# Two chained feed-forward layers behind pooled attention: matmuls that read each stream by turns from its two halves

## The chip, the cores and the metric

The kernel runs on one core of a Trainium2 chip. The metric is the device time of one execution in microseconds (us); the kernel before takes 964.29 us, the median of three runs (964.23 to 964.79).

## What is computed

12480 tokens of 128 features go through an attention with 32 inducing points, then through two feed-forward layers of width 2048, all in float32:

```python
h = mab(I, x)                     # 32 rows: softmax(scale * I x^T) x
x = mab(x, h)                     # 12480 rows: softmax(scale * x h^T) h
h1 = x @ w_in;  x = maximum(0.01 * h1, h1) @ w_out
h2 = x @ w2_in; x = (h2 * sigmoid(1.702 * h2)) @ w2_out
```

## The kernel before, in words

Tokens are the columns everywhere: a tile of tokens is 128 partitions (features, or rows of attention weights) by 512 columns. There are 25 such tiles; the last two in the order of work have 352 columns. The first 40 us or so pool the tokens into the 32 rows (transposes, scores, a running softmax). Then come two layers of 25 tiles by 16 steps, 800 steps in all, in the order of the list `steps`: layer 1 for all tiles, then layer 2 for all tiles, and within a tile the 16 blocks f of 128 hidden features. The program is written out in that order by hand; `extra` hangs other work (weight conversion, attention weights of later tiles, splitting) on chosen steps.

One step has three parts. `ffn_in` multiplies a block of the first matrix with the tile's stream into a PSUM tile `h_ps`; `ffn_act` applies the nonlinearity and splits the result into two float32r streams `ghi` (rounded) and `glo` (the rest); `ffn_out`, three steps later (`LOOK`), multiplies them with the second matrix and adds to the tile's PSUM tile `acc`. A product of two float32 factors is made of three float32r matmuls: high by high, low by high, high by low.

- Layer 1, inward: one matmul (L774), `hw` by `at`. The attention is folded into the first matrix (`hw`), and the stream `at` holds the attention weights of the tile's tokens; for the first two tiles ScalarE writes it (L580), for the others `stack` loads it with four DMAs (L662), ten steps before it is first read.
- Layer 1, activation: ScalarE's relu writes `ghi` (L788), VectorE writes `glo` (L789).
- Layer 2, inward: three matmuls (L778, L779, L780) on `x2h` and `x2l`, which `halves` splits from the first layer's result (L514 on ScalarE, L515 on VectorE).
- Layer 2, activation: ScalarE's silu (L794) and its rounding copy `ghi` (L795), VectorE's `glo` (L796).
- Outward, both layers: L806, L807 (both on `ghi`) and L808 (on `glo`); at the last step of a tile of layer 1 one more, `lin` by `at` (L810), which carries the 0.01 part of the first nonlinearity.
- `ffn_end` copies `acc` out: in layer 1 to `x2` on ScalarE (L824); in layer 2 to `o_t` on VectorE (L832), for the very last tile on ScalarE (L829), followed by the store.

In a matmul the streamed operand (`at`, `x2h`, `x2l`, `ghi`, `glo`) is called the stream or moving operand here, the matrix block that is loaded into the array the weights. All streams are read in the order of their columns.

Of the kernel before, what the change touches and what calls it, by code (L numbers as in the profile page):

```python
# [10 lines left out]
F32 = mybir.dt.float32  # L11
F32R = mybir.dt.float32r
U32 = mybir.dt.uint32
BF16 = mybir.dt.bfloat16
AF = mybir.ActivationFunctionType
# [3 lines left out]
P = 128  # L19
LOOK = 3  # L20
# [37 lines left out]
def kernel(  # L58
# [12 lines left out]
    nc = tc.nc  # L71
    _, N, C = x.shape
    m = inducing.shape[0]
    DFF = moe_w_in.shape[1]
    NF = DFF // P
    TOK = TC * P
# [3 lines left out]
    tok = [TC * k for k in ch]  # L80
# [7 lines left out]
    const = ctx.enter_context(tc.tile_pool(name="const", bufs=1))  # L88
# [151 lines left out]
    while len(early) < len(order):  # L240
# [6 lines left out]
        out=sel, in_=ident.rearrange("p (q k) -> p k q", q=NQ), axis=AX.X, op=ALU.add  # L247
# [7 lines left out]
        out=quad, in_=ident.rearrange("p (q k) -> p q k", q=NQ), axis=AX.X, op=ALU.add  # L255
# [6 lines left out]
    l = xnp.tile([P, NP], F32, name="l")  # L262
# [7 lines left out]
    def slot(t, dtype, name):  # L270
        return slots.tile([P, TOK], dtype, tag=f"slot{t}", name=f"{name}{t}")
# [151 lines left out]
    for i in range(NP - 1):  # L423
# [10 lines left out]
        j = 0 if i == 1 else i - 2 if i >= 3 else None  # L434
# [69 lines left out]
    main = ctx.enter_context(tc.tile_pool(name="main", bufs=2))  # L504
# [2 lines left out]

    main.tile([P, 112], F32, tag="gap", name="gap", bufs=1)

    def halves(src, name, pool=const, tag=None):  # L510
        shape = list(src.shape)
        hi = pool.tile(shape, F32R, name=f"{name}h", tag=f"{tag or name}h")
        lo = pool.tile(shape, F32R, name=f"{name}l", tag=f"{tag or name}l")
        nc.scalar.activation(out=hi, in_=src, func=AF.Copy)  # L514
        nc.vector.tensor_tensor(out=lo, in0=src, in1=hi.bitcast(F32), op=ALU.subtract)  # L515
        return hi, lo


    at_t = {}

    def weights_tile():


        return main.tile([P, TOK], F32R, tag="at", name="at", bufs=3)

    def token_tile(t, rest):

        st = {}
        n = ch[t]
        bc = lambda v: v.rearrange("p (j u) -> p j u", u=1).to_broadcast([n, TC, m])  # L530
        tiny = lambda name: main.tile([P, TC], F32, tag=name, name=name, bufs=2)[:n]

        def s0():
            ps = ps_h.tile([P, 512], F32, tag="h", name="s2_ps")
            for k in range(TC):
                nc.tensor.matmul(
                    ps[:n, k * m : (k + 1) * m], xT[t][:, k * n : (k + 1) * n],
                    hT[:, 0, :], start=True, stop=True,
                )
            st["ps"] = ps  # L540

        def s0b():
            ps = st["ps"]
            sv = ps[:n, : TC * m].rearrange("p (j k) -> p j k", j=TC)
            mxt = tiny("nmx")
            nc.vector.tensor_reduce(out=mxt, in_=sv, axis=AX.X, op=ALU.max)
            a = main.tile([P, TC, m], F32, tag="na", name="na", bufs=2)[:n]
            nc.vector.tensor_tensor(out=a, in0=sv, in1=bc(mxt), op=ALU.subtract)
            nc.scalar.activation(out=a, in_=a, func=AF.Exp, scale=SCALE)
            st["a"] = a  # L550

        def s1():
            a = st["a"]
            sst = tiny("nsum")
            nc.vector.tensor_reduce(out=sst, in_=a, axis=AX.X, op=ALU.add)
            nc.vector.tensor_scalar_add(sst, sst, EPS)
            nc.vector.reciprocal(sst, sst)
            nc.vector.tensor_tensor(out=a, in0=a, in1=bc(sst), op=ALU.mult)

        def s2():  # L560
            a = st["a"]
            rows = main.tile([P, TC, NQ, m], F32R, tag="rows", name="rows", bufs=2)[:n]
            dup = lambda v: v.rearrange("p j (u k) -> p j u k", u=1).to_broadcast(
                [n, TC, 2, m]
            )
            hi, lo = rows[:, :, 0:NQ:2, :], rows[:, :, 1:NQ:2, :]
            nc.vector.tensor_copy(hi, dup(a))
            rest.tensor_tensor(out=lo, in0=dup(a), in1=hi.bitcast(F32), op=ALU.subtract)
            st["rows"] = rows

        def s3():
            ps = ps_h.tile([P, 512], F32, tag="h", name="rows_ps")
            for k in range(TC):
                nc.tensor.transpose(
                    ps[:, k * n : (k + 1) * n],
                    st["rows"][:, k].rearrange("p q k -> p (q k)").bitcast(F32),
                    ident[:n, :n],
                )
            at_t[t] = weights_tile()[:, : tok[t]]
            nc.scalar.activation(out=at_t[t], in_=ps[:, : tok[t]], func=AF.Copy)  # L580

        return [s0, s0b, s1, s2, s3]

    NG = (NT - 2 + NQ - 1) // NQ
    hl = [None] * NG
# [71 lines left out]

    def stack(t):
        g, q = divmod(t - 2, NQ)
        a = weights_tile()[:, : tok[t]]  # L660
        for k in range(NQ):
            nc.sync.dma_start(  # L662
                out=a[k * m : (k + 1) * m, :].bitcast(F32),
                in_=hl[g][k % 2][q * m : (q + 1) * m, : tok[t]],
            )
        at_t[t] = a

# [12 lines left out]
    hw = wts.tile([P, DFF], F32R, name="hw")  # L680
# [32 lines left out]
    lin = const.tile([P, C], F32R, name="lin")  # L713
# [48 lines left out]
    x2_t = {}  # L762
    x2h_t = {}
    h_t = {}
    g_t = {}
    acc_t = {}
    late = {}

    def ffn_in(l, t, f):
        ps = ps_h.tile([P, 512], F32, tag="h", name="h_ps")  # L770
        o = ps[:, : tok[t]]
        cols = slice(f * P, (f + 1) * P)
        if l == 0:
            nc.tensor.matmul(o, hw[:, cols], at_t[t], start=True, stop=True)  # L774
        else:
            hi, lo = x2h_t[t]
            wh, wl = late["w2"]
            nc.tensor.matmul(o, wh[:, cols], hi, start=True, stop=False)  # L778
            nc.tensor.matmul(o, wl[:, cols], hi, start=False, stop=False)  # L779
            nc.tensor.matmul(o, wh[:, cols], lo, start=False, stop=True)  # L780
        h_t[l, t, f] = o

    def ffn_act(l, t, f):
        o = h_t.pop((l, t, f))
        hi = main.tile([P, TOK], F32R, tag="ghi", name="ghi", bufs=LOOK + 2)[:, : tok[t]]
        lo = main.tile([P, TOK], F32R, tag="glo", name="glo", bufs=LOOK + 2)[:, : tok[t]]
        if l == 0:
            nc.scalar.activation(out=hi, in_=o, func=AF.Relu)  # L788
            nc.vector.scalar_tensor_tensor(  # L789
                out=lo, in0=o, scalar=0.0, in1=hi.bitcast(F32), op0=ALU.max, op1=ALU.subtract  # L790
            )
        else:
            g = main.tile([P, TOK], F32, tag="g", name="g")[:, : tok[t]]
            nc.scalar.activation(out=g, in_=o, func=AF.Silu, scale=BETA)  # L794
            nc.scalar.activation(out=hi, in_=g, func=AF.Copy)  # L795
            nc.vector.tensor_tensor(out=lo, in0=g, in1=hi.bitcast(F32), op=ALU.subtract)  # L796
        g_t[l, t, f] = (hi, lo)

    def ffn_out(l, t, f):
        hi, lo = g_t.pop((l, t, f))  # L800
        if f == 0:
            acc_t[l, t] = ps_a.tile([P, 512], F32, tag="a", name="acc")
        o = acc_t[l, t][:, : tok[t]]
        v = v1 if l == 0 else late["v2"]
        end = l == 1 and f == NF - 1
        nc.tensor.matmul(o, v[:, f, 0, :], hi, start=(f == 0), stop=False)  # L806
        nc.tensor.matmul(o, v[:, f, 1, :], hi, start=False, stop=False)  # L807
        nc.tensor.matmul(o, v[:, f, 0, :], lo, start=False, stop=end)  # L808
        if l == 0 and f == NF - 1:
            nc.tensor.matmul(o, lin, at_t.pop(t), start=False, stop=True)  # L810

    def x2_slot(t):

# [6 lines left out]
    def ffn_end(l, t):  # L820
        ps = acc_t.pop((l, t))[:, : tok[t]]
        if l == 0:
            x2_t[t] = slot(x2_slot(t), F32, "x2")[:, : tok[t]]
            nc.scalar.activation(out=x2_t[t], in_=ps, func=AF.Copy, scale=1.0 - LEAK)  # L824
        else:
            o = main.tile([P, TOK], F32, tag="o", name="o_t")[:, : tok[t]]
            dst = outT[:, col[t] : col[t] + tok[t]]
            if t == NT - 1:
                nc.scalar.activation(out=o, in_=ps, func=AF.Copy, scale=1.0 / BETA)  # L829
                nc.scalar.dma_start(out=dst, in_=o)  # L830
            else:
                nc.vector.tensor_scalar_mul(o, ps, 1.0 / BETA)  # L832
                nc.sync.dma_start(out=dst, in_=o)

    steps = [(l, t, f) for l in range(2) for t in range(NT) for f in range(NF)]
    steps[: 2 * NF] = [(0, t, 4 * b + f) for b in range(NF // 4) for t in (0, 1) for f in range(4)]
# [69 lines left out]
    def split_x2(t):  # L906

        if not gaps:
            gaps.append(main.tile([P, 96], F32, tag="gap2", name="gap2", bufs=1))
        x2h_t[t] = halves(x2_t.pop(t), "x2", main)  # L910

    for t in range(NT):
        at(NT * NF + (t - 1) * NF + 6, split_x2, t)
# [1 line left out]
    for n in range(len(steps) + LOOK):  # L915
# [3 lines left out]
        if n >= LOOK:  # L919
            l, t, f = steps[n - LOOK]  # L920
# [44 lines left out]
```

## Time and profile before

| what | value |
|---|---|
| median of three runs | 964.29 us (964.23 to 964.79) |
| profiled execution, first to last instruction (its span) | 962.6 us |
| TensorE busy | 953.7 us (99%) |
| TensorE loading weights | 779.5 us (81%) |
| ScalarE busy | 783.0 us (81%) |
| VectorE busy | 631.5 us (66%) |
| GpSimd busy | 52.8 us (5%) |

The page gives the span as the profiled execution's own time. A matmul's record lasts from its start until its last result is written; records overlap, so how fast TensorE works is read from the distance between starts. PEld is the loading of weights, which runs beside the matmul before it. The granted clock is a share of TensorE's full 2.4 GHz; the lower of its two levels is 1.2 GHz. A chain of waits is followed back from the last instruction to what released each step.

### The profile page before, as it was taken

How to read it: one execution, taken by the hardware profiler on the slowest of the kernel's cores; microseconds unless marked ns; L12 is line 12 of the kernel's file. 1: busy time of each engine (PE TensorE's matmuls, PEld its weight loads, DVE VectorE, ACT ScalarE, POOL GpSimd, SP SyncE). 2: the span in 40 equal slices, each digit the busy share in tenths (PEclk: the TensorE clock that was granted, in tenths of full speed). 3: DMA queues.
4: the chain of work that ended last, by engine and by line, in shares of the span. 5: the costliest groups of instructions: out<-in, count | busy, mean ns of one | idle time of the engine just before them, and what ended most of it. 6: DMA issues, size and time to landing. Idle time of an engine off the chain costs nothing.

```text
span 962.6 us, 13196 instructions
## 1 busy us (share of the span) xinstructions
PE 953.7 (99%) x4577; PEld 779.5 (81%) x4577; DVE 631.5 (66%) x1002; ACT 783.0 (81%) x1357; POOL 52.8 (5%) x64
## 2 busy tenths in 40 slices
PE   8999999999999999999999999999999999999998
PEld 6677787887878878898888888888888888888888
DVE  3897788878878777765555555555555555555554
ACT  6666777767767666689999999999999999999998
POOL 1330101102100010000000000000000000000000
PEclk9999999999999999999999999999999999999999
DMA  9302120021000000000000000000000000000000
GB/s 337 107 1 55 34 66 23 20 81 33 23 22 12 23 12 19 8 1 12 12 12 12 12 11 12 15 19 12 12 11 12 12 12 12 12 12 23 12 12 16
DMA packets 15334, 27.90 MB, mean 29 GB/s; under 512 B 2347, under 2 KB 6987, under 8 KB 15267
## 3 DMA queue, kind: packets, MB, share of 16 engines
q1 hardware_dynamic: 15123, 26.88, 9.0%
q8 instruction: 36, 0.59, 0.3%
q14 instruction: 31, 0.25, 0.1%
q10 hardware_dynamic: 144, 0.18, 0.1%
HBM read 14.79 MB, written 6.39 MB: 22 GB/s over the span
## 4 chain that ended last, share of the span: by engine, by line
PE 94%; DVE 3%; DMA 1%; ACT 1%; issue 0%; POOL 0%; SPq 0%; ACTq 0%; POOLq 0%
PE acc L806 18%; PE acc L808 18%; PE acc L807 18%; PE h_ps L778 9%; PE h_ps L780 9%; PE h_ps L779 9%; PE h_ps L774 9%; DVE glo L789 1%; DMA xn<-in_x_dram 1%; PE s_ps L609 1%; PE xT_ps L279 1%; PE acc L810 1%; PE pv_ps L348 0%; DVE v L158 0%; DVE v L153 0%
## 5 line engine op out<-in xcount | busy, mean ns | idle before, releaser
L796 DVE TENSOR_TENSOR glo<-g,ghi 128x512 fp32r<-128x512 f32 (+1 forms) x400 | 271.7, 679 | 236.8 <-ACT ghi L795 223.2
L788 ACT ACTIVATE ghi<-h_ps 128x512 fp32r<-128x512 f32 (+1 forms) x400 | 232.2, 587 | 97.8 <-PE h_ps L774 96.2
L806 PE MATMUL acc<-ghi,v 128*128 128x512 f32 (+1 forms) x800 | 309.8, 387 | 0.0
L789 DVE SCALAR_TENSOR_TENSOR glo<-h_ps,ghi 128x512 fp32r<-128x512 f32 (+1 forms) x400 | 264.4, 674 | 68.8 <-ACT ghi L788 63.8
L808 PE MATMUL acc<-glo,v 128*128 128x512 f32 (+1 forms) x800 | 309.2, 386 | 0.1
L807 PE MATMUL acc<-ghi,v 128*128 128x512 f32 (+1 forms) x800 | 307.5, 384 | 0.0
L794 ACT ACTIVATE g<-h_ps 128x512 f32<-128x512 f32 (+1 forms) x400 | 234.3, 586 | 33.7 <-PE h_ps L780 0.6
L795 ACT ACTIVATE ghi<-g 128x512 fp32r<-128x512 f32 (+1 forms) x400 | 248.4, 621 | 12.7
L808 PEld LDWEIGHTS acc<-glo,v 128*128 128x128 f32 x800 | 150.2, 188 | 32.2 <-DVE glo L789 0.6
L807 PEld LDWEIGHTS acc<-ghi,v 128*128 128x128 f32 x800 | 150.2, 188 | 30.5
L806 PEld LDWEIGHTS acc<-ghi,v 128*128 128x128 f32 x800 | 150.3, 188 | 28.6 <-issue 0.2
L774 PE MATMUL h_ps<-at,hw 128*128 128x512 f32 (+1 forms) x400 | 155.7, 390 | 0.0
L778 PE MATMUL h_ps<-x2h,w2h 128*128 128x512 f32 (+1 forms) x400 | 155.3, 388 | 0.0
L780 PE MATMUL h_ps<-x2l,w2h 128*128 128x512 f32 (+1 forms) x400 | 154.5, 386 | 0.0
L779 PE MATMUL h_ps<-x2h,w2l 128*128 128x512 f32 (+1 forms) x400 | 153.1, 383 | 0.0
L774 PEld LDWEIGHTS h_ps<-at,hw 128*128 128x128 f32 x400 | 75.1, 188 | 18.8 <-issue 3.8
L780 PEld LDWEIGHTS h_ps<-x2l,w2h 128*128 128x128 f32 x400 | 75.1, 188 | 16.2
L779 PEld LDWEIGHTS h_ps<-x2h,w2l 128*128 128x128 f32 x400 | 75.1, 188 | 15.5
L778 PEld LDWEIGHTS h_ps<-x2h,w2h 128*128 128x128 f32 x400 | 75.2, 188 | 13.8
L824 ACT ACTIVATE x<-acc 128x512 f32<-128x512 f32 (+1 forms) x25 | 14.7, 587 | 7.6 <-PE acc L810 7.6
L515 DVE TENSOR_TENSOR x2l<-x,x2h 128x512 fp32r<-128x512 f32 (+1 forms) x25 | 16.8, 672 | 0.0
L283 ACT ACTIVATE xT<-xT_ps 128x512 f32<-128x512 f32 (+1 forms) x25 | 12.7, 586 | 4.6 <-PE xT_ps L279 4.6
(111 smaller groups left out, 312.7 us busy)
## 6 DMA issues: line engine op xcount, KB each, us to landing
out_dram<-o_t SPq DMA_DIRECT2D x23, 256.0 KB, 2.0
xn<-in_x_dram SPq DMA_DIRECT2D x11, 512.0 KB, 9.3
raw<-in_moe_w_in_dram SPq DMA_DIRECT2D x8, 512.0 KB, 5.3
raw<-in_moe_w_out_dram SPq DMA_DIRECT2D x8, 512.0 KB, 4.8
at<-hlhi SPq DMA_DIRECT2D x42, 64.0 KB, 2.0
at<-hllo SPq DMA_DIRECT2D x42, 64.0 KB, 2.0
xn<-in_x_dram SPq DMA_DIRECT2D x1, 352.0 KB
xn<-in_x_dram SPq DMA_DIRECT2D x1, 256.0 KB, 12.4
```

Of the source, the lines that this page charges most:

```text
L774: nc.tensor.matmul(o, hw[:, cols], at_t[t], start=True, stop=True)
L778: nc.tensor.matmul(o, wh[:, cols], hi, start=True, stop=False)
L779: nc.tensor.matmul(o, wl[:, cols], hi, start=False, stop=False)
L780: nc.tensor.matmul(o, wh[:, cols], lo, start=False, stop=True)
L788: nc.scalar.activation(out=hi, in_=o, func=AF.Relu)
L789: nc.vector.scalar_tensor_tensor(out=lo, in0=o, scalar=0.0, in1=hi.bitcast(F32), op0=ALU.max, op1=ALU.subtract)
L794: nc.scalar.activation(out=g, in_=o, func=AF.Silu, scale=BETA)
L795: nc.scalar.activation(out=hi, in_=g, func=AF.Copy)
L796: nc.vector.tensor_tensor(out=lo, in0=g, in1=hi.bitcast(F32), op=ALU.subtract)
L806: nc.tensor.matmul(o, v[:, f, 0, :], hi, start=(f == 0), stop=False)
L807: nc.tensor.matmul(o, v[:, f, 1, :], hi, start=False, stop=False)
L808: nc.tensor.matmul(o, v[:, f, 0, :], lo, start=False, stop=end)
```

## The change

Each stream's tile is seen as two halves, `[128, 2, 256]` (for tiles of 352 columns, 176 columns of each half are used, so the second half still begins 256 words, 1 KB, behind the first). ScalarE, VectorE and the loads write it as before, first half then second (`runs`). The matmuls read column 0 of the first half, column 0 of the second, column 1 of the first, and so on (`turns`), and write the products to PSUM one after the other. So each product leaves the columns shuffled: old column i * n/2 + j stands at 2j + i. A column's place is thereby doubled, modulo n - 1; after four products (inward and outward in two layers) it is 16 times the old one, and the copy of a tile's end in layer 2 puts the columns back in order by reading PSUM with a step of 16. The matmul with `lin` has one stream between `at` and `acc` where the others have two, so it reads `at` in the order of two shuffles. `hw`, the weights, the number of instructions and their order on every engine stay as they are.

```diff
@@ -507,10 +507,26 @@
 
     main.tile([P, 112], F32, tag="gap", name="gap", bufs=1)
 
-    def halves(src, name, pool=const, tag=None):
-        shape = list(src.shape)
-        hi = pool.tile(shape, F32R, name=f"{name}h", tag=f"{tag or name}h")
-        lo = pool.tile(shape, F32R, name=f"{name}l", tag=f"{tag or name}l")
+    def stream(name, bufs, t):
+        s = main.tile([P, 2, TOK // 2], F32R, tag=name, name=name, bufs=bufs)
+        return s[:, :, : tok[t] // 2]
+    def runs(ap):
+        return ap.rearrange("p (i j) -> p i j", i=2)
+    def turns(s):
+        return s.rearrange("p i j -> p j i")
+    def pairs(ap):
+        return ap.rearrange("p (j i) -> p j i", i=2)
+    def halves(src, t):
+        hi = stream("x2h", 2, t)
+        lo = stream("x2l", 2, t)
+        src = runs(src)
         nc.scalar.activation(out=hi, in_=src, func=AF.Copy)
         nc.vector.tensor_tensor(out=lo, in0=src, in1=hi.bitcast(F32), op=ALU.subtract)
         return hi, lo
@@ -518,10 +534,8 @@
 
     at_t = {}
 
-    def weights_tile():
-        return main.tile([P, TOK], F32R, tag="at", name="at", bufs=3)
+    def weights_tile(t):
+        return stream("at", 3, t)
 
     def token_tile(t, rest):
 
@@ -576,8 +590,8 @@
                     st["rows"][:, k].rearrange("p q k -> p (q k)").bitcast(F32),
                     ident[:n, :n],
                 )
-            at_t[t] = weights_tile()[:, : tok[t]]
-            nc.scalar.activation(out=at_t[t], in_=ps[:, : tok[t]], func=AF.Copy)
+            at_t[t] = weights_tile(t)
+            nc.scalar.activation(out=at_t[t], in_=runs(ps[:, : tok[t]]), func=AF.Copy)
 
         return [s0, s0b, s1, s2, s3]
 
@@ -657,11 +671,11 @@
 
     def stack(t):
         g, q = divmod(t - 2, NQ)
-        a = weights_tile()[:, : tok[t]]
+        a = weights_tile(t)
         for k in range(NQ):
             nc.sync.dma_start(
-                out=a[k * m : (k + 1) * m, :].bitcast(F32),
-                in_=hl[g][k % 2][q * m : (q + 1) * m, : tok[t]],
+                out=a[k * m : (k + 1) * m].bitcast(F32),
+                in_=runs(hl[g][k % 2][q * m : (q + 1) * m, : tok[t]]),
             )
         at_t[t] = a
 
@@ -770,44 +784,49 @@
         ps = ps_h.tile([P, 512], F32, tag="h", name="h_ps")
         o = ps[:, : tok[t]]
         cols = slice(f * P, (f + 1) * P)
+        h_t[l, t, f] = runs(o)
+        o = pairs(o)
         if l == 0:
-            nc.tensor.matmul(o, hw[:, cols], at_t[t], start=True, stop=True)
+            nc.tensor.matmul(o, hw[:, cols], turns(at_t[t]), start=True, stop=True)
         else:
-            hi, lo = x2h_t[t]
+            hi, lo = map(turns, x2h_t[t])
             wh, wl = late["w2"]
             nc.tensor.matmul(o, wh[:, cols], hi, start=True, stop=False)
             nc.tensor.matmul(o, wl[:, cols], hi, start=False, stop=False)
             nc.tensor.matmul(o, wh[:, cols], lo, start=False, stop=True)
-        h_t[l, t, f] = o
 
     def ffn_act(l, t, f):
         o = h_t.pop((l, t, f))
-        hi = main.tile([P, TOK], F32R, tag="ghi", name="ghi", bufs=LOOK + 2)[:, : tok[t]]
-        lo = main.tile([P, TOK], F32R, tag="glo", name="glo", bufs=LOOK + 2)[:, : tok[t]]
+        hi = stream("ghi", LOOK + 2, t)
+        lo = stream("glo", LOOK + 2, t)
         if l == 0:
             nc.scalar.activation(out=hi, in_=o, func=AF.Relu)
             nc.vector.scalar_tensor_tensor(
                 out=lo, in0=o, scalar=0.0, in1=hi.bitcast(F32), op0=ALU.max, op1=ALU.subtract
             )
         else:
-            g = main.tile([P, TOK], F32, tag="g", name="g")[:, : tok[t]]
+            g = runs(main.tile([P, TOK], F32, tag="g", name="g")[:, : tok[t]])
             nc.scalar.activation(out=g, in_=o, func=AF.Silu, scale=BETA)
             nc.scalar.activation(out=hi, in_=g, func=AF.Copy)
             nc.vector.tensor_tensor(out=lo, in0=g, in1=hi.bitcast(F32), op=ALU.subtract)
-        g_t[l, t, f] = (hi, lo)
+        g_t[l, t, f] = (turns(hi), turns(lo))
 
     def ffn_out(l, t, f):
         hi, lo = g_t.pop((l, t, f))
         if f == 0:
             acc_t[l, t] = ps_a.tile([P, 512], F32, tag="a", name="acc")
-        o = acc_t[l, t][:, : tok[t]]
+        o = pairs(acc_t[l, t][:, : tok[t]])
         v = v1 if l == 0 else late["v2"]
         end = l == 1 and f == NF - 1
         nc.tensor.matmul(o, v[:, f, 0, :], hi, start=(f == 0), stop=False)
         nc.tensor.matmul(o, v[:, f, 1, :], hi, start=False, stop=False)
         nc.tensor.matmul(o, v[:, f, 0, :], lo, start=False, stop=end)
         if l == 0 and f == NF - 1:
-            nc.tensor.matmul(o, lin, at_t.pop(t), start=False, stop=True)
+            nc.tensor.matmul(
+                acc_t[l, t][:, : tok[t]].rearrange("p (a c i) -> p a c i", c=2, i=2), lin,
+                at_t.pop(t).rearrange("p c (i a) -> p a c i", i=2), start=False, stop=True,
+            )
 
     def x2_slot(t):
 
@@ -823,14 +842,16 @@
             x2_t[t] = slot(x2_slot(t), F32, "x2")[:, : tok[t]]
             nc.scalar.activation(out=x2_t[t], in_=ps, func=AF.Copy, scale=1.0 - LEAK)
         else:
-            o = main.tile([P, TOK], F32, tag="o", name="o_t")[:, : tok[t]]
+            o_t = main.tile([P, TOK], F32, tag="o", name="o_t")[:, : tok[t]]
+            o = o_t.rearrange("p (b a) -> p b a", b=16)
+            ps = ps.rearrange("p (a b) -> p b a", b=16)
             dst = outT[:, col[t] : col[t] + tok[t]]
             if t == NT - 1:
                 nc.scalar.activation(out=o, in_=ps, func=AF.Copy, scale=1.0 / BETA)
-                nc.scalar.dma_start(out=dst, in_=o)
+                nc.scalar.dma_start(out=dst, in_=o_t)
             else:
                 nc.vector.tensor_scalar_mul(o, ps, 1.0 / BETA)
-                nc.sync.dma_start(out=dst, in_=o)
+                nc.sync.dma_start(out=dst, in_=o_t)
 
     steps = [(l, t, f) for l in range(2) for t in range(NT) for f in range(NF)]
     steps[: 2 * NF] = [(0, t, 4 * b + f) for b in range(NF // 4) for t in (0, 1) for f in range(4)]
@@ -907,7 +928,7 @@
 
         if not gaps:
             gaps.append(main.tile([P, 96], F32, tag="gap2", name="gap2", bufs=1))
-        x2h_t[t] = halves(x2_t.pop(t), "x2", main)
+        x2h_t[t] = halves(x2_t.pop(t), t)
 
     for t in range(NT):
         at(NT * NF + (t - 1) * NF + 6, split_x2, t)
```

## Rows read from the trace of the kernel before

**Rows 1.** The page, parts 1 and 2: busy us (share), instructions; granted clock in tenths.

```profile
span 962.6 us, 13196 instructions
...
PE 953.7 (99%) x4577; PEld 779.5 (81%) x4577; DVE 631.5 (66%) x1002; ACT 783.0 (81%) x1357; POOL 52.8 (5%) x64
...
PEclk9999999999999999999999999999999999999999
```

**Rows 2.** The page, part 4: shares of the chain that ended last, by engine and line.

```profile
PE 94%; DVE 3%; DMA 1%; ACT 1%; issue 0%; POOL 0%; SPq 0%; ACTq 0%; POOLq 0%
PE acc L806 18%; PE acc L808 18%; PE acc L807 18%; PE h_ps L778 9%; PE h_ps L780 9%; PE h_ps L779 9%; PE h_ps L774 9%; DVE glo L789 1%; DMA xn<-in_x_dram 1%; PE s_ps L609 1%; PE xT_ps L279 1%; PE acc L810 1%; PE pv_ps L348 0%; DVE v L158 0%; DVE v L153 0%
```

**Rows 3.** Timeline, 700 to 706 us: start us, us, engine, line, operation, tiles, shape.

```profile
700.06 0.39 PE L806 MATMUL acc<-ghi,v 128*128 128x512 f32 x1
...
705.56 0.39 PE L806 MATMUL acc<-ghi,v 128*128 128x512 f32 x1
```

**Rows 4.** Timeline of TensorE, 935 to 938 us.

```profile
934.80 0.32 PE L806 MATMUL acc<-ghi,v 128*128 128x352 f32 x1
...
937.68 0.32 PE L806 MATMUL acc<-ghi,v 128*128 128x352 f32 x1
```

**Rows 5.** Groups of TensorE by shape: xcount | busy us, mean ns | idle before.

```profile
L806 PE MATMUL acc<-ghi,v 128*128 128x512 f32 x736 | 289.1, 393 | 0.0
...
L774 PE MATMUL h_ps<-at,hw 128*128 128x512 f32 x368 | 145.3, 396 | 0.0
...
L806 PE MATMUL acc<-ghi,v 128*128 128x352 f32 x64 | 20.6, 323 | 0.0
...
L690 PE MATMUL hw_ps<-w,hT 128*128 128x512 f32 x8 | 4.2, 625 | 0.1
```

**Rows 6.** Timelines of TensorE at 5, 20, 40 and 69 us.

```profile
5.51 0.49 PE L118 MATMUL idle_ps<-idle 128*128 128x256 bf16 x3
...
20.27 0.60 PE L329 MATMUL p_ps<-ident,e_t 128*128 128x128 f32 x4
...
39.94 1.96 PE L690 MATMUL hw_ps<-w,hT 128*128 128x512 f32 x4
...
42.41 0.28 PE L118 MATMUL idle_ps<-idle 128*128 128x256 bf16 x1
...
69.10 0.63 PE L732 MATMUL lin_ps<-v,hwT 128*128 128x256 f32 x4
```

**Rows 7.** Timeline at 0 to 3 us; then groups of ScalarE, 100 to 400 us.

```profile
1.34 0.37 DVE L246 TENSOR_REDUCE sel<-ident 128x32 f32<-128x128 f32 x1 [0.21 <-POOL ident masks.py:199]
...
1.89 0.28 DVE L254 TENSOR_REDUCE quad<-ident 128x4 f32<-128x128 f32 x1
...
L147 ACT ACTIVATE v<-raw 128x512 f32<-128x512 f32 x8 | 5.3, 661 | 0.0
L629 ACT ACTIVATE a<-a 128x512 f32<-128x512 f32 (+1 forms) x5 | 3.1, 625 | 0.0
```

**Rows 8.** Windows: us, busy us (x) of PE, PEld, DVE, ACT, POOL, clock, DMA, GB/s.

```profile
40.00:60.00 20.00, 19.16 (x97) 13.17 (x97) 17.84 (x38) 15.00 (x29) 5.01 (x6) 1.00 0.00 1
60.00:80.00 20.00, 19.16 (x91) 14.98 (x91) 18.44 (x33) 12.70 (x24) 6.25 (x6) 1.00 0.06 14
...
200.00:300.00 100.00, 100.00 (x444) 80.23 (x443) 81.27 (x129) 71.48 (x124) 14.74 (x14) 1.00 0.11 27
...
700.00:800.00 100.00, 100.00 (x438) 82.04 (x438) 55.61 (x82) 90.78 (x151) 0.00 (x0) 1.00 0.03 11
```

**Rows 9.** Groups of VectorE, 500 to 900 us; then the timeline of the end.

```profile
L832 DVE TENSOR_SCALAR o_t<-acc 128x512 f32<-128x512 f32 x18 | 12.3, 683 | 0.0
...
958.68 0.43 PE L808 MATMUL acc<-glo,v 128*128 128x352 f32 x1
959.15 0.46 ACT L829 ACTIVATE o_t<-acc 128x352 f32<-128x352 f32 x1 [1.08 <-PE acc L808]
```

**Rows 10.** The page, part 6: out<-in, queue, operation xcount, KB each, us to landing.

```profile
at<-hlhi SPq DMA_DIRECT2D x42, 64.0 KB, 2.0
```

## The prediction

> **What bounds the kernel now.** I read the page's busy times first: TensorE is busy 99% of the 962.6 us span, ScalarE 81%, VectorE 66%, and the granted clock is full in every slice, the 2.4 GHz level [rows 1]. The chain of waits agrees: 94% of the time to the end is TensorE, nearly all of it seven lines, the matmuls of the two layers [rows 2]. A busy TensorE is not a TensorE at its peak, so the timeline comes next, read for the distance from one start to the next. L806 stands once in every six matmuls of layer 2; from 700.06 to 705.56 us lie four such steps, 5.50 / 24 = 0.229 us per matmul of 512 columns [rows 3]. In the two tiles of 352 columns three steps take 2.88 us, 0.160 us per matmul [rows 4]. At 2.4 GHz, one column a cycle, they would take 0.2133 and 0.1467. So each pays 15.7 and 13.3 ns more than its columns, and between the two lengths a column costs 69 / 160 = 0.431 ns where the clock gives 0.417: about half of the excess grows with the columns.
>
> Counts: per layer 1 step one product in (L774) and three out; per layer 2 step three and three; one L810 per tile. With 736 of L806 and 368 of L774 at 512 columns [rows 5] that is 3 x 736 + 4 x 368 + 23 = 3703 matmuls, and with 64 of L806 and half as many of each inward line at 352, 3 x 64 + 4 x 32 + 2 = 322. They fill 3703 x 0.229 + 322 x 0.160 = 899.5 us. The profiled span lies 1.7 us under the median of the runs, 964.29; I work with differences and set them against the median.
>
> Where does the excess come from? Other streams tell. A single record of 256 columns lasts 0.28 us, so three bf16 ones in 0.49 follow each other every 0.105 us, the clock's 0.107 within the table's rounding; four float32r ones of 256 in 0.63 every 0.117, 10 ns more; float32 transposes of 128 columns take 0.107, twice the columns' time, with no excess, though each loads new weights [rows 6]. Bf16 asks its store for 2 bytes a column at full pace, float32 for 4 at half pace, both 4.8 bytes per ns and partition; only float32r asks for 9.6, and only it pays. That points at the reading of the moving stream, not at weights, waits or the array.
>
> **The change part by part.** It adds and removes no instruction and moves none: each engine issues the same operations in the same order, and what each adds to a queue is nothing.
>
> *The 4025 matmuls* read column by column from two places 1 KB apart, each place in order, and write to PSUM one after the other as before. If the two halves can be read side by side, each is asked for 4.8 bytes per ns, the rate at which the bf16 and float32 rows show no excess. Bounds: the best is the clock itself, 15.7 x 3703 + 13.3 x 322 ns = 62 us less. On the bad side no matmul of this kernel steps through its stream, so the nearest rows are far. ScalarE reading every second word takes 661 ns for 512 where neighbours take 625: 36 ns more, 3703 x 36 + 322 x 25 ns = 141 us. VectorE's reduction that jumps 128 bytes at every element takes 0.37 us against 0.28 for 128 elements in order, 0.7 ns per element [rows 7], though it also writes eight times as many results: 360 x 3703 + 248 x 322 ns = 1413 us. Between them stands TensorE at half pace: float32 records of 512 columns follow every (1.96 - 0.62) / 3 = 0.45 us [rows 5, 6], which would add 221 x 3703 + 149 x 322 ns = 866 us. I take a pace 3.2 ns above the clock, near the bf16 row: 216.5 and 150 ns. That saves 12.5 x 3703 + 10 x 322 ns = 49.5 us.
>
> The Trainium skill (TensorE: Matmul & The Clock Gate, section Back-to-back issue gap) gives a warm matmul its columns at 2.4 GHz plus 2.5 ns; the rows above show 15.7, so for this stream the trace differs. By its price, 215.8 ns, the saving would be some 52 us, an estimate from that page.
>
> *What is not gained.* From 40 to 80 us 188 matmuls start and VectorE is busy 17.8 and 18.4 us of 20 [rows 8], with its L789 on the chain [rows 2]; there I leave TensorE's saving out: 188 x 12.5 ns = 2.4 us.
>
> *The engines behind.* In layer 2 ScalarE is busy 90.8% of a step of 6 x 0.229 = 1.373 us, so 1.247 us [rows 8]; the step becomes 1.299, and ScalarE 96% busy, still behind TensorE, with three steps of look-ahead against a burst. In layer 1 VectorE needs 0.813 x 0.917 = 0.745 us of a step that becomes 0.866. Both hide; ScalarE is late next, and under 0.208 us per matmul it would be the bound.
>
> *The writers* of the streams (L580, L788 to L796, L514, L515) write the same elements one after the other; at 352 columns in two runs of 176. Nothing; if that cover is gone, it is ScalarE's 4% that goes first. *The 84 loads of at* (L662) carry the same 64 KB in two runs, and land after 2.0 us [rows 10]; they are issued ten steps, about 9 us, ahead. Nothing.
>
> *The last copy* of a tile reads PSUM with a step of 16 words. On VectorE it takes 683 ns now [rows 9]; between no change and 0.7 ns per element it becomes up to 1.04 us, once in 22 us, on an engine that is 56% busy [rows 8]; behind it waits one glo, which TensorE needs three steps later. Nothing. The very last, on ScalarE, 0.46 us, lies on the path between the last matmul and the last store [rows 9]: 0 to 0.25 us by the same row; I take 0.1, since ScalarE's own stepped row costs little.
>
> Sum: -49.5 + 2.4 + 0.1 = -47.0 us, **917.3 us**.
>
> **The rivals.** *Only part goes* (chance 0.25): if turns help the part that grows with the columns but not a matmul's start, 7.5 ns of 512 and 5.2 of 352 go, 29 us, less 1.4 in the early stretch: 936; anything from 930 to 962 belongs here. For it: the excess has a fixed part of about 8 ns, which a change of order within a stream need not touch. Against: the float32 rows start as often and pay none.
>
> *No change* (0.10): the excess is not in the reading, or the halves lie in one place for the chip and are fetched ahead anyway: 964.4. For it: 229 ns holds for every line and buffer alike, as if fixed by something that no address touches.
>
> *Slower* (0.20): the store hands over several neighbouring words at a time and a column out of turn begins anew. Then each matmul of the layers lengthens at its own place, TensorE's reading; it decides from 0.447 ns per column on, that is as soon as a turn costs more than the 0.03 ns per column now lost. At half pace the time is 964 + 866 = 1830 us; with the mild price 1105; with VectorE's 2377. For it: both stepped rows are dearer than their neighbours. Against: each of two places is read in order, so what was fetched serves the next columns if two such pieces are held. I give half pace or worse 0.14, the mild price 0.06.
>
> The Trainium skill has this as a rule (Advanced Engine Details and Errata, section SBUF Cachelines): SBUF has lines of 16 bytes, at least two accesses in a row must hit one to hide its latency, and another line at every access costs. By that rule the time is this rival's; the stepped rows agree with it in sign, and no matmul here shows it.
>
> **How the numbers follow.** The forecast near full pace has 0.45. Faster: 0.45 + 0.25 = 0.70; within 0.2% (1.9 us, about what a measurement of this kernel can tell from no change): 0.10; slower: 0.20. The likeliest is 917. The range: 902 is the clock itself, and the bf16 row makes its last 6 us unlikely, so 908 below; the cases faster and unchanged hold 0.80 together, so it ends at 966 and the slower ones are left out.
>
> **What would show it.** Right: L806 every 1.30 us in layer 2, 0.87 in layer 1, a mean of a matmul unchanged but more starts per 100 us (about 462 instead of 438), ScalarE at 96% in layer 2 and still not on the chain. Wrong: a step of 1.37 us (no change), of 2.7 us (half pace), or a step held by ScalarE with TensorE idle before L778. VectorE's last copy much over 1.04 us, or a last ScalarE copy over 0.71, would show a dearer PSUM step than I take.

## The result, and the profile after

The changed kernel takes **917.58 us**, the median of four runs (917.34 to 918.42), against 964.27 us for the kernel before (964.23 to 964.79): a ratio of 0.9515, 95% interval 0.9502 to 0.9529. The forecast of 917.3 us holds; the reason that it gave holds only in part, as the experiments show.

The page of the changed kernel, parts 1, 2 and 4:

```profile
span 915.2 us, 13207 instructions
...
PE 905.5 (99%) x4577; PEld 780.3 (85%) x4577; DVE 631.5 (69%) x1002; ACT 777.7 (85%) x1357; POOL 52.9 (6%) x64
...
PEclk9999999999999999999999999999999999999999
...
PE 95%; DVE 4%; ACT 1%; issue 1%; POOL 0%; ACTq 0%; POOLq 0%; DVEq 0%
```

Beside [rows 1, 2] little seems to have happened: TensorE is busy 99% as before, with as many matmuls at the same granted clock (the 11 more instructions in the total are none of the engines' counted work), and 95% of the chain is still its own. A busy share doesn't tell that each matmul became shorter. The timeline does. L821 is the old L806; first TensorE at 700 to 706 us, then its two tiles of 352 columns (columns as in [rows 3]):

```profile
699.89 0.38 PE L821 MATMUL acc<-ghi,v 128*128 128x512 f32 x1
...
701.19 0.38 PE L821 MATMUL acc<-ghi,v 128*128 128x512 f32 x1
...
705.07 0.38 PE L821 MATMUL acc<-ghi,v 128*128 128x512 f32 x1
...
890.54 0.31 PE L821 MATMUL acc<-ghi,v 128*128 128x352 f32 x1
...
892.33 0.31 PE L821 MATMUL acc<-ghi,v 128*128 128x352 f32 x1
```

From 699.89 to 705.07 lie four steps of six matmuls: 5.18 / 24 = 0.2158 us each, where [rows 3] gave 0.229. In the short tiles 1.79 / 12 = 0.149 us, where [rows 4] gave 0.160. The columns alone take 0.2133 and 0.1467 at 2.4 GHz, so 2.5 ns above the clock is left of 15.7, and of 13.3.

The windows of the changed kernel, columns as in [rows 8]:

```profile
40.00:60.00 20.00, 18.95 (x97) 12.92 (x97) 17.69 (x37) 14.63 (x28) 4.49 (x5) 1.00 0.00 1
60.00:80.00 20.00, 17.97 (x88) 14.08 (x87) 18.67 (x32) 12.49 (x25) 6.69 (x6) 1.00 0.06 14
200.00:300.00 100.00, 100.00 (x468) 85.22 (x467) 86.41 (x138) 75.00 (x131) 14.77 (x14) 1.00 0.11 28
700.00:800.00 100.00, 100.00 (x465) 87.58 (x464) 59.01 (x88) 95.80 (x161) 0.00 (x0) 1.00 0.04 14
```

In 100 us of layer 2 stand 465 matmuls instead of 438, and ScalarE fills 95.8 us instead of 90.8. From 40 to 80 us nothing is gained: 185 matmuls against 188. Over the first 100 us the windows of both kernels count the same 717 matmuls, 199 of them of layer 1.

**Where the time came from.** After those 100 us stand 3504 matmuls of 512 columns and 322 of 352. Between 500 and 850 us the starts lie 228.9 ns apart on average in the kernel before and 215.8 in the changed one, 13.1 ns less; the short ones lie 11 ns closer. That gives 45.9 + 3.5 = 49.4 us. One group gives something back, the matmul with `lin`; the groups of TensorE by shape, columns as in [rows 5], first that of the kernel before, then those of the changed one, then the changed one's timeline:

```profile
L810 PE MATMUL acc<-at,lin 128*128 128x512 f32 x23 | 9.0, 391 | 0.0
...
L823 PE MATMUL acc<-glo,v 128*128 128x512 f32 x736 | 279.7, 380 | 0.5 <-DVE glo L804 0.4
L821 PE MATMUL acc<-ghi,v 128*128 128x512 f32 x736 | 279.0, 379 | 0.0
...
L826 PE MATMUL acc<-at,lin 128*128 128x512 f32 x23 | 10.2, 445 | 0.0
...
200.01 0.44 PE L826 MATMUL acc<-at,lin 128*128 128x512 f32 x1
200.29 0.38 PE L790 MATMUL h_ps<-at,hw 128*128 128x512 f32 x1
```

Its record grew from 391 ns to 445 while the others fell to 379; by starts it holds TensorE 0.28 us (200.01 to the next start at 200.29). Instead of saving 13 ns it costs some 50: 66 ns x 20 after those 100 us, with its two short ones some 1.4 us. That leaves 48.0 us. The spans differ by 47.4 (962.6 and 915.2). The last 0.6 us may be TensorE's weight loads for L823, which after 100 us wait 0.9 us in all for VectorE's `glo`, where those of the kernel before (L808) wait 0.2.

The copies that put the columns in order, from the groups of VectorE and the timeline of the end, columns as in [rows 9]:

```profile
L853 DVE TENSOR_SCALAR o_t<-acc 128x512 f32<-128x512 f32 x23 | 15.7, 684 | 0.0
...
911.35 0.42 PE L823 MATMUL acc<-glo,v 128*128 128x352 f32 x1
911.80 0.47 ACT L850 ACTIVATE o_t<-acc 128x352 f32<-128x352 f32 x1 [1.07 <-PE acc L823]
```

684 and 465 ns stand against 683 and 464 before: reading PSUM with a step of 16 words costs nothing on either engine.

### The profile page after: what moved, and what is told of

Its sections match the earlier page's. It is cut to its first block, busy times and chain, and to the rows that moved or that the text cites. A ratio compares the mean times of both kernels' runs of the same rounds, so it can differ in the third digit from the quotient of the medians.

```text
span 915.2 us, 13207 instructions
## 1 busy us (share of the span) xinstructions
PE 905.5 (99%) x4577; PEld 780.3 (85%) x4577; DVE 631.5 (69%) x1002; ACT 777.7 (85%) x1357; POOL 52.9 (6%) x64
## 4 chain that ended last, share of the span: by engine, by line
PE 95%; DVE 4%; ACT 1%; issue 1%; POOL 0%; ACTq 0%; POOLq 0%; DVEq 0%
PE acc L823 18%; PE acc L821 18%; PE acc L822 18%; PE h_ps L796 9%; PE h_ps L795 9%; PE h_ps L794 9%; PE h_ps L790 9%; DVE glo L804 1%; PE xT_ps L279 1%; PE acc L826 1%; PE s_ps L623 1%; PE idle_ps L118 1%; PE pv_ps L348 0%; DVE v L158 0%; DVE pT_t L338 0%
## 5 line engine op out<-in xcount | busy, mean ns | idle before, releaser
L823 PE MATMUL acc<-glo,v 128*128 128x512 f32 (+1 forms) x800 | 299.9, 375 | 0.5 <-DVE glo L804 0.4
L821 PE MATMUL acc<-ghi,v 128*128 128x512 f32 (+1 forms) x800 | 299.2, 374 | 0.0
L822 PE MATMUL acc<-ghi,v 128*128 128x512 f32 (+1 forms) x800 | 298.9, 374 | 0.0
L804 DVE SCALAR_TENSOR_TENSOR glo<-h_ps,ghi 128x512 fp32r<-128x512 f32 (+1 forms) x400 | 261.6, 674 | 51.9 <-ACT ghi L803 48.1
L823 PEld LDWEIGHTS acc<-glo,v 128*128 128x128 f32 x800 | 151.2, 189 | 23.0 <-DVE glo L804 3.1
L821 PEld LDWEIGHTS acc<-ghi,v 128*128 128x128 f32 x800 | 151.3, 189 | 21.3 <-ACT ghi L803 0.4
L790 PE MATMUL h_ps<-at,hw 128*128 128x512 f32 (+1 forms) x400 | 150.8, 378 | 0.0
L794 PE MATMUL h_ps<-x2h,w2h 128*128 128x512 f32 (+1 forms) x400 | 149.5, 374 | 0.0
L796 PE MATMUL h_ps<-x2l,w2h 128*128 128x512 f32 (+1 forms) x400 | 149.5, 374 | 0.0
L795 PE MATMUL h_ps<-x2h,w2l 128*128 128x512 f32 (+1 forms) x400 | 149.5, 374 | 0.0
```

The lines of the kernel that those rows point to most:

```text
L790: nc.tensor.matmul(o, hw[:, cols], turns(at_t[t]), start=True, stop=True)
L804: nc.vector.scalar_tensor_tensor(out=lo, in0=o, scalar=0.0, in1=hi.bitcast(F32), op0=ALU.max, op1=ALU.subtract)
```

## The experiments

The distance from one start to the next is the measure throughout, in ns for 512 columns. A record's own length moves with it: 379 ns belong to starts 216 apart, 394 to 229 or so, 630 to about 440. Four kernels try eight orders at once: on tiles of 512 columns, step f of a tile reads its streams in order number f % 8, each order from a source line of its own so that the trace keeps them apart. They write the products to PSUM one after the other, so columns of different blocks get mixed and the sums are not those of the layers; tiles of 352 columns keep their turns. Their total times only sum up eight orders and come from one run each. For them the distances are medians from layer 2, between two matmuls of the same order that follow each other (46 distances for each place that such a pair has in a step), and a range is given where the places differ. The pair right behind a slower order is 18 to 37 ns longer; it is left out for the orders that are not themselves slow.

**1. Is it the reading by turns, or something else in the change?** The changed kernel, with the halves read one after the other and everything else left in place:

```diff
     def turns(s):
-        return s.rearrange("p i j -> p j i")
+        return s
     def pairs(ap):
-        return ap.rearrange("p (j i) -> p j i", i=2)
+        return ap.rearrange("p (i j) -> p i j", i=2)
...
-                acc_t[l, t][:, : tok[t]].rearrange("p (a c i) -> p a c i", c=2, i=2), lin,
-                at_t.pop(t).rearrange("p c (i a) -> p a c i", i=2), start=False, stop=True,
+                pairs(acc_t[l, t][:, : tok[t]]), lin,
+                turns(at_t.pop(t)), start=False, stop=True,
...
-            o = o_t.rearrange("p (b a) -> p b a", b=16)
-            ps = ps.rearrange("p (a b) -> p b a", b=16)
+            o = o_t
```

> The changed kernel with its tiles of two halves, but every matmul reads the first half and then the second, and the last copy reads in order; all else as changed. Theory A (the gain is the reading by turns alone): 512 columns every 229 ns again, 963 to 966 us, equal to the kernel before. Rival B (the layout of the tiles or the copies took part in the gain): between 918 and 960 us, matmuls at less than 229 ns.

964.61 us, ratio 1.0001 (0.9991 to 1.001). Its timeline of TensorE:

```profile
700.46 0.39 PE L821 MATMUL acc<-ghi,v 128*128 128x512 f32 x1
...
705.95 0.39 PE L821 MATMUL acc<-ghi,v 128*128 128x512 f32 x1
```

5.49 / 24 = 229 ns. The new tiles, loads and writers are worth nothing; the order of reading is all of the gain.

**2. Must the two places lie far apart?** Blocks of 2d words, each read by turns from its two halves, with distances d of 1 (plain order), 4, 8, 16, 32, 64, 128 and 256 words:

```diff
+        d = [1, 4, 8, 16, 32, 64, 128, 256][k]
+        return ap.rearrange("p (b i j) -> p b j i", i=2, j=d)
```

> The columns of full tiles are read by turns from two places that lie 4, 8, 16, 32, 64, 128 or 256 words apart (blocks f = 1 to 7 modulo 8; f = 0 reads in plain order), so the columns of different blocks are mixed and the sums are not those of the layers. Each distance has a line of its own. Theory A1 (two places are read side by side only if they lie in different parts of the store): near distances stay at 229 ns or are worse, from some distance on 216 ns. Rival A2 (a piece of neighbouring words is held for each place and alternating as such helps): 216 ns from 4 words on, at every distance. Rival C (every step to another 16 byte line costs, and 256 words is an exception): over 229 ns for 4 to 128 words, 300 ns or more. A record lasts some 160 ns longer than the distance of starts: 374 ns where it is 216, 392 where it is 229.

923.12 us. Groups of TensorE by shape; L541 is the plain order, L543 a distance of 4 words, L555 of 256:

```profile
L541 PE MATMUL acc<-ghi,v 128*128 128x512 f32 x184 | 57.5, 394 | 0.0
...
L555 PE MATMUL acc<-ghi,v 128*128 128x512 f32 x184 | 54.7, 379 | 0.0
...
L543 PE MATMUL acc<-ghi,v 128*128 128x512 f32 x184 | 54.7, 379 | 0.0
```

All seven distances have 379 ns and starts 216 apart; the plain order has 394 and 230 to 235. (The 374 of the expectation is a mean over both shapes.) The alternation as such counts (A2), and 16 bytes are far enough. That the gain needs two distant places (A1), my prediction's picture, falls, and so does C.

**3. Do more places help further?** Turns over n = 2, 4, 8 to 256 places, 512 / n words each:

```diff
+        n = [2, 4, 8, 16, 32, 64, 128, 256][k]
+        return ap.rearrange("p (i j) -> p j i", i=n)
```

> The columns of full tiles are read by turns from 2, 4, 8, 16, 32, 64, 128 or 256 places (blocks f = 0 to 7 modulo 8), evenly spread over the tile, so the columns of different blocks are mixed and the sums are not those of the layers. 256 places are steps of two words, 128 of four. Theory A (pieces are held for a few places and fetched side by side): 2 places 216 ns, 4 places about 280 as the matmul with lin shows in the changed kernel (275 to 286 ns to the next start), from 8 on some constant, half pace or worse (450 ns and more), since a piece is gone when its next word is asked for; 256 places cheaper than 128, two words of a piece being read one after the other. Rival D (the number of places does not matter, the matmul with lin is slow for another reason): 216 ns for all up to 64 places. Total under A: 1300 to 2300 us.

1606.17 us. Groups by shape; L541 has two places, L543 four, L545 eight, L551 sixty-four, L555 256 (step 8 bytes):

```profile
L545 PE MATMUL acc<-ghi,v 128*128 128x512 f32 x184 | 115.2, 724 | 0.0
L555 PE MATMUL acc<-ghi,v 128*128 128x512 f32 x184 | 100.4, 638 | 0.0
...
L551 PE MATMUL acc<-ghi,v 128*128 128x512 f32 x184 | 94.1, 601 | 0.0
L543 PE MATMUL acc<-ghi,v 128*128 128x512 f32 x184 | 67.7, 451 | 0.0
L541 PE MATMUL acc<-ghi,v 128*128 128x512 f32 x184 | 56.7, 389 | 0.0
```

By starts: 216 with two places (234 to 247 right behind a slower order, hence the 389), 273 to 287 with four, 536 to 548 with eight, 414 to 465 from sixteen on. Of the numbers tried, only two is good. The prediction's slower rival thus exists, one step of the same kind further on. Why eight places are worse than sixteen no run here settles.

**4. What does the reading of `at` from four places cost?** Three kernels on one chip: the changed kernel again; L826 reading two places as the others do, so that the 0.01 part lands on the wrong columns; and L826 as two matmuls of 256 columns that each read two places and write every second pair of PSUM columns.

> The changed kernel itself, beside the next two: 917 to 918.5 us.

```diff
-                acc_t[l, t][:, : tok[t]].rearrange("p (a c i) -> p a c i", c=2, i=2), lin,
-                at_t.pop(t).rearrange("p c (i a) -> p a c i", i=2), start=False, stop=True,
+                pairs(acc_t[l, t][:, : tok[t]]), lin,
+                turns(at_t.pop(t)), start=False, stop=True,
```

> The matmul with lin reads its stream from two places like the others, so the 0.01 part of the first layer lands on the wrong columns; nothing else changes. Theory A (four places cost 60 to 70 ns more than two): its records fall from 445 to 375 ns, 25 x 0.06 = 1.5 us less than the changed kernel, 916 us. Rival E (those 60 ns are hidden behind the wait for the copy of acc that follows): no difference, 917.5 us.

```diff
-            nc.tensor.matmul(
-                acc_t[l, t][:, : tok[t]].rearrange("p (a c i) -> p a c i", c=2, i=2), lin,
-                at_t.pop(t).rearrange("p c (i a) -> p a c i", i=2), start=False, stop=True,
-            )
+            to = acc_t[l, t][:, : tok[t]].rearrange("p (a c i) -> p c a i", c=2, i=2)
+            by = at_t.pop(t).rearrange("p c (i a) -> p c a i", i=2)
+            nc.tensor.matmul(to[:, 0], lin, by[:, 0], start=False, stop=False)
+            nc.tensor.matmul(to[:, 1], lin, by[:, 1], start=False, stop=True)
```

> The matmul with lin is cut into two of 256 columns, each reading by turns from two places 128 words apart and writing pairs of columns four words apart in PSUM. Theory A (two places at this distance are as good as at 256 words, and pairs cost nothing in PSUM): two records of 109 ns to the next start, 218 instead of about 280 ns, 1.5 us less than the changed kernel, 916 us. Rival F (stepped pairs in PSUM slow the matmul): 280 ns or more, 917.5 us or slower.

| kernel | median us | runs | ratio to before |
|---|---|---|---|
| changed | 917.76 | 917.45 to 917.86 | 0.9517 (0.9504 to 0.953) |
| `lin`: two places | 916.01 | 915.8 to 916.29 | 0.95 (0.9487 to 0.9513) |
| `lin` in two halves | 916.44 | 916.18 to 916.49 | 0.9503 (0.9491 to 0.9516) |

The four places cost 917.76 - 916.01 = 1.75 us, where starts alone gave 1.4 for 22 of the 25. The kernel with two halves gets 1.3 of it back. The ratios' intervals overlap; on this one chip every run of the two variants is under every run of the changed kernel, but the variants' own runs overlap. The kernel with two halves is the fastest version here that leaves nothing out. Its timeline of TensorE:

```profile
199.89 0.27 PE L828 MATMUL acc<-at,lin 128*128 128x256 f32 x1
200.00 0.28 PE L829 MATMUL acc<-at,lin 128*128 128x256 f32 x1
200.11 0.38 PE L790 MATMUL h_ps<-at,hw 128*128 128x512 f32 x1
```

0.11 us for each 256 columns is full pace, so writing PSUM in pairs of words with gaps of two costs nothing.

**5. Is it the number of words in a row?** Two places in turn, r = 2, 4, 8 to 128 words at each; the eighth order, in the changed kernel's terms, is 0, 2, 1, 3 in every four words:

```diff
+        if k == 7:
+            return ap.rearrange("p (b i j) -> p b j i", i=2, j=2)
+        r = [2, 4, 8, 16, 32, 64, 128][k]
+        return ap.rearrange("p (i b j) -> p b i j", i=2, j=r)
```

> Full tiles are read by turns from the two halves again, but 2, 4, 8, 16, 32, 64 or 128 words in a row from each before the other has its turn (blocks f = 0 to 6 modulo 8); f = 7 reads words 0, 2, 1, 3 of every four, so both places lie in one piece of 16 bytes. The columns of different blocks are mixed, so the sums are not those of the layers. Theory G (a place's next piece must be fetched while the other place is read, so each column has to change place, or nearly): 216 ns for 2 in a row, 229 from 4 words, a whole piece of 16 bytes, on; 229 for words 0, 2, 1, 3. Rival H (a stream described as one plain run of 512 is what is slow, and any stream described in turns is fast): 216 ns in all eight. Rival I (the time is lost where a run goes on from one piece to the next in the store, so each break saves): 216 at 2, then rising evenly towards 229 as the runs get longer.

1036.75 us. Groups by shape; L545 has two words in a row, L547 four, L557 128, L559 is 0, 2, 1, 3:

```profile
L545 PE MATMUL acc<-ghi,v 128*128 128x512 f32 x184 | 75.9, 498 | 0.0
L547 PE MATMUL acc<-ghi,v 128*128 128x512 f32 x184 | 60.8, 413 | 0.0
...
L557 PE MATMUL acc<-ghi,v 128*128 128x512 f32 x184 | 58.2, 398 | 0.0
L559 PE MATMUL acc<-ghi,v 128*128 128x512 f32 x184 | 56.8, 390 | 0.0
```

By starts: 321 to 333 with two in a row, 240 to 255 with four, 226 to 243 from eight on; 226 to 229 for 0, 2, 1, 3. H and I fall. G came nearest, but it had 216 for two in a row. A single series of words per matmul hardly explains places that are good one word at a time and bad two at a time. That led to theory K: **even and odd columns are fetched as two series, and each series wants as many words in a row as possible out of one piece of 16 bytes.** Turns between two places give each series four such words, the plain order two, two words at a time from two places a to-and-fro.

**6. Does the start of a stream matter?** The kernel before, with 32 more bytes ahead of all its streams (rival J):

```diff
-    main.tile([P, 112], F32, tag="gap", name="gap", bufs=1)
+    main.tile([P, 120], F32, tag="gap", name="gap", bufs=1)
```

> The kernel before with every stream tile 32 bytes further on in its partition (the unused tile gap has 120 words, not 112), so streams begin at a multiple of 512 bytes and not 32 bytes ahead of one. Theory G (the loss is one of reading piece after piece in order, wherever it starts): 229 ns as before, 963 to 966 us. Rival J (the loss comes from where a stream begins): another pace, at least 2 ns per matmul to either side, 7 us of the total.

981.39 us (980.83 to 981.45), ratio 1.0177 (1.016 to 1.0194), 17 us slower. Timeline of TensorE:

```profile
700.42 0.40 PE L806 MATMUL acc<-ghi,v 128*128 128x512 f32 x1
...
704.62 0.40 PE L806 MATMUL acc<-ghi,v 128*128 128x512 f32 x1
```

4.20 / 18 = 233 ns instead of 229. J holds for the plain order.

**7. Theory K against orders that tell it apart** (rival M). Order 0 is the turns; 1 to 3 turn between two places but walk each in steps of 2, 4 and 8 words; 4 reads each column twice, so that both series walk through the same words; 5 is 0, 1, 4, 5, 8, 9 and so on, two in a row for the stream but one per series; 6 is 0, 2, 4, 6, 1, 3, 5, 7; 7 is plain:

```diff
+        if k == 0:
+            return ap.rearrange("p (i j) -> p j i", i=2)
+        if k < 4:
+            return ap.rearrange("p (i j s) -> p s j i", i=2, s=2 ** k)
+        if k == 4:
+            return ap[:, :256].rearrange("p (j i) -> p j i", i=1).to_broadcast([P, 256, 2])
+        if k == 5:
+            return ap.rearrange("p (b i r) -> p i b r", i=2, r=2)
+        if k == 6:
+            return ap.rearrange("p (b j i) -> p b i j", b=64, i=2)
+        return ap
```

> Again eight orders in one run on full tiles, blocks f = 0 to 7 modulo 8, columns of different blocks mixed, sums not those of the layers. Theory K, formed on the runs so far: the columns are fetched in two interleaved series, the even and the odd ones, and each series wants to take four words in a row from one 16 byte piece; two in a row are just too few, one is half pace, whatever the other series does. f = 0: turns of two halves (four in a row per series) 216 ns. f = 1, 2, 3: turns of two halves in steps of 2, 4 and 8 words (two, one, one in a row) 229 to 235, then 433 to 470 twice. f = 4: each column of one half read twice, one after the other (four in a row) 216. f = 5: words 0, 1, 4, 5, 8, 9 and so on, then the pairs left out (one in a row per series, two in a row for the stream) 433 to 470. f = 6: words 0, 2, 4, 6, 1, 3, 5, 7 of every eight (each series goes to and fro between two pieces) 280 to 330. f = 7: in order (two in a row) 229. Rival M (it helps that a column lies in another piece than the column before): f = 0 to 3 all 216, f = 4 at 229 or slower, f = 5 about 325 as for two words in a row from two halves.

1316.39 us. Timeline of TensorE; L561 is order 1, L563 order 2, L567 order 4, L569 order 5, L571 order 6, always the second and third of a step's inward matmuls:

```profile
701.78 0.39 PE L561 MATMUL h_ps<-x2h,w2l 128*128 128x512 f32 x1
702.00 0.40 PE L561 MATMUL h_ps<-x2l,w2h 128*128 128x512 f32 x1
...
703.70 0.63 PE L563 MATMUL h_ps<-x2h,w2l 128*128 128x512 f32 x1
704.15 0.64 PE L563 MATMUL h_ps<-x2l,w2h 128*128 128x512 f32 x1
...
707.55 0.38 PE L567 MATMUL h_ps<-x2h,w2l 128*128 128x512 f32 x1
707.77 0.38 PE L567 MATMUL h_ps<-x2l,w2h 128*128 128x512 f32 x1
...
709.12 0.65 PE L569 MATMUL h_ps<-x2h,w2l 128*128 128x512 f32 x1
709.59 0.64 PE L569 MATMUL h_ps<-x2l,w2h 128*128 128x512 f32 x1
...
711.76 0.51 PE L571 MATMUL h_ps<-x2h,w2l 128*128 128x512 f32 x1
712.10 0.51 PE L571 MATMUL h_ps<-x2l,w2h 128*128 128x512 f32 x1
```

| order | words in a row, per series and 16 bytes | ns between starts |
|---|---|---|
| 0 turns; 4 each column twice | 4 | 216; 216 |
| 1 turns, step 2; 7 plain | 2 | 226 to 233; 226 to 233 |
| 2, 3 turns, steps 4 and 8; 5 | 1 | 442 to 455, 440 to 462; 433 to 471 |
| 6: two, then back for the others | to and fro | 334 to 350 |

K called seven of eight in advance, to within 3 ns of its ranges, and the last (280 to 330) too low. Order 5 tells most: two neighbours at a time from every piece of 16 bytes run at half the pace, as K says of a series that gets one word per piece. M falls.

**8. Is the changed kernel free of the start?** The 32 bytes of experiment 6, now in the changed kernel; by K four words in a row leave no edge to stumble on:

> The changed kernel with every stream tile 32 bytes further on, the shift that made the kernel before 17 us slower. Theory K (turns leave each series time to spare, so where a stream begins matters no more): 917 to 918.5 us, 216 ns per matmul. Rival N (the start of a stream costs what it costs in any order): some 4 ns per matmul more, 930 to 936 us.

917.54 us (917.2 to 918.14), ratio 0.9511 (0.9495 to 0.9527). Timeline of TensorE:

```profile
700.72 0.38 PE L821 MATMUL acc<-ghi,v 128*128 128x512 f32 x1
...
705.90 0.38 PE L821 MATMUL acc<-ghi,v 128*128 128x512 f32 x1
```

5.18 / 24 = 216 ns, as without the shift. In the plain order this shift cost 17 us; with the turns it costs nothing. No other shift was tried.

## Why the prediction was right, point by point

- **What bounds the kernel**: right. TensorE was the bound in both layers after 100 us, and distances between starts, not busy shares or records, held the 15.7 ns.
- **Where the excess lies, "the reading of the moving stream"**: right, shown by experiment 1 and by every order tried since.
- **How the turns help, "if the two halves can be read side by side, each is asked for 4.8 bytes per ns"**: this step of the reasoning failed. Two places 16 bytes apart do as well (experiment 2); four places, asked for half as much each, are slower than the plain order (273 to 287); and the order that reads each column twice runs at 216 from one place, though it also asks for only half as many different words. By theory K what counts is how many words in a row each series of columns, even or odd, gets from one piece of 16 bytes: four 216, two 226 to 255, one 414 to 471, to and fro between two pieces 273 to 350. All orders of experiments 2, 3, 5 and 7 but the eight places fit that; that the chip has two such readers is inferred from them, not seen.
- **The pace, 216.5 and 150 ns**: 215.8 and 149.0, mis-sized by 0.7 and 1.0 ns, 2.9 us too little gained over 4025 matmuls. The Trainium skill's price (TensorE: Matmul & The Clock Gate, section Back-to-back issue gap), columns at 2.4 GHz plus 2.5 ns, is what the changed kernel measures, 215.8; the kernel before doesn't.
- **"What is not gained", 2.4 us between 40 and 80 us**: right in kind, and near in size by luck. The 188 are all matmuls of that stretch, and only 116 of them are the layers'; but nothing is gained up to 100 us, which is 199 of the layers' matmuls, 2.6 us at 13.1 ns.
- **"The 4025 matmuls read column by column from two places"**: wrong for 25 of them. In the order of two shuffles the matmul with `lin` reads four places, as the diff shows, and this term, taken as a saving, costs 1.75 us (experiment 4). With the last 0.6 us above, and with 0.4 us because the pace before is 228.9 and not 229.0 ns, this offsets the better pace. That 917.3 came so close to 917.58 is in part luck.
- **The engines behind**: right. ScalarE 95.8% busy against 96% forecast, TensorE without a gap; 465 starts per 100 us against 462. One sign of being right failed: "a mean of a matmul unchanged". The mean record of L806 was 393 ns [rows 5], that of L821 is 379, so a record's length does follow the pace of the reading.
- **The last copies**: nothing where 0 to 0.36 and 0 to 0.25 us were allowed. VectorE's row L246 [rows 7] didn't carry over to a step in PSUM, and the 0.1 us on the path isn't there (0.47 against 0.46).
- **The rival "only part goes"**: didn't happen; of its fixed 8 ns all but 2.5 went as well (15.7 and 13.3 ns above the clock became 2.5 at both lengths), so they belonged to the reading too.
- **The rival "no change"**: didn't happen. Its evidence, "as if fixed by something that no address touches", fell by itself: 32 bytes move the plain order from 229 to 233 (experiment 6). Nor did 229 ns quite hold "for every line" before: by the trace the median distance behind L779 is 226 and behind L778 232.
- **The slower rival**: didn't happen here, but other orders show its price. Orders in which a series gets one word per piece take 414 ns and more (experiments 3 and 7), as if each such column began anew. What kept this change clear of it fits the sentence given against it, that "what was fetched serves the next columns if two such pieces are held". The Trainium skill's rule (Advanced Engine Details and Errata, section SBUF Cachelines), at least two accesses in a row per 16-byte line, would have forbidden the turns and passed order 5. The trace agrees with the piece of 16 bytes; the count goes per series, and two are not quite enough, 229 against 216.

## What to carry to other kernels

Where float32r matmuls bound a kernel and their starts lie more than the columns apart, let the moving operand be read by turns from two places, even 16 bytes apart (0, 4, 1, 5, 2, 6, 3, 7), write PSUM in order, and undo the shuffle in a copy that some engine makes anyway. Don't let two products' shuffles add up in one read, since four places already cost more than none; split that matmul instead. And judge TensorE by the distance between starts: its busy share was 99% before and after 47 us had gone.

## What was not expected of the hardware

- Even and odd columns of a float32r stream behave as two readers: the order 0, 1, 4, 5 takes 433 to 471 ns for 512 columns, 0, 4, 1, 5 takes 216.
- Two words at a time from two places take 321 to 333 ns, more than one word at a time (216) and more than four (240 to 255).
- Eight places (536 to 548) are slower than sixteen (433 to 439); why stays open.
- In the plain order the start of a stream counts, 229 or 233 ns with 32 bytes between them, and with turns this shift makes no difference (215.8 ns in both).
- PSUM can be read with a step of 64 bytes by VectorE (684 ns, 683 in order) and ScalarE (465, 464), and written in spaced pairs by TensorE (0.11 us for 256 columns), at no cost.
